# A grouped-query attention block with a cached K and V: TensorE's batches 8 to 31 as a hardware loop with counted-down semaphores and fixed buffer slots

## The chip, the cores and the metric

The kernel runs on one core of one Trainium2 chip. The metric is the device time of one execution in microseconds (us). Five runs of the kernel before took between 367.18 and 367.44 us, with a median of 367.32. A profile is one further execution; its span is the time from the first to the last instruction on the core.

The engines are named as in the profile: PE is TensorE's matmul row and PEld its weight loads, DVE is VectorE, ACT ScalarE, POOL GpSimd, and SP SyncE, whose queue issues the DMA transfers.

## The reference

```python
B, Sq, D, Hq, Hkv, Sk, Dh = 32, 4, 1024, 32, 4, 2048, 128
q = (x @ wq).reshape(B, Sq, Hq, Dh).transpose(0, 2, 1, 3)
k = jnp.repeat(k_cache, rep, axis=1)          # k_cache, v_cache: [B, Hkv, Sk, Dh]
v = jnp.repeat(v_cache, rep, axis=1)
scores = jnp.einsum("bhqd,bhkd->bhqk", q, k) * (Dh ** -0.5)
p = _softmax(scores, axis=-1)
o = jnp.einsum("bhqk,bhkd->bhqd", p, v)
return o.transpose(0, 2, 1, 3).reshape(B, Sq, Hq * Dh) @ wo
```

All tensors are bfloat16. Each batch has 2 MB of K and 2 MB of V; wq and wo have 8 MB each. With the 64 cache tiles that is about 151 MB read from memory, once.

## The kernel before, in words

The program is written as a list of operations for each engine (class `_Program`). Every operation may name what it waits for and what it completes. `emit` turns a wait into "semaphore of the producing engine at least n", where n is the producer's place in that engine's count: counters only ever rise, each engine has one, and each buffer slot has one for its DMA. `emit` writes every engine's stream straight out, so PE's code holds each matmul of all 32 batches.

Buffers. `big` has eight slots of 2 MB. At first four of them hold wq; then all K and V tiles run through the slots as a ring, in the order of the list `loads`: three K tiles ahead, then K of batch b+3 (b+4 from batch 17 on) and V of batch b in turn. A load waits for the last user of its slot: a K tile is free after its last transpose `("kt", b, 3)`, a V tile after its last matmul `("pv", b)`. From batch 10 on one slot is taken out of the ring and serves as a second P buffer (`PF_sb`), cleared by ACT; until then there is one (`PD_sb`). At the end the four chunks of wo use the slots that come free next. SP issues all loads in the order of the list, so a load that waits holds up all behind it.

Per batch i the work is:

- `qd` (L277, POOL): four copies put the queries of batch i in block-diagonal form into `QD_sb`;
- `kt` (L286, DVE): four transposes of K chunks into one of two halves of `KT_sb`;
- `pe_qk` (L298 for the matmul with a weight load, L16 for those that keep the weights): 16 matmuls into `ps_s`, which has one buffer, so they wait for `exp` of the batch before;
- `softmax_max` (L306, L307, DVE): the row maximum and its negative scaling;
- `softmax_exp` (L311, ACT): exp from `ps_s` into `P_sb`, with the row sum;
- `pt` (L319, L320, DVE): the transpose of P into `PT_sb` and the reciprocal of the sum;
- `pd` (L332, POOL): four copies into `PD_sb` or `PF_sb`, block-diagonal;
- `pe_pv` (L341, PE): 64 matmuls of P with V into `ps_r`, then `o_evac` (L348, ACT), `pe_ot` (L359, PE) and `ot_evac` (L364, ACT).

Iteration i of the main loop, which runs in Python and is written out in full, emits `qd` and two of the four `kt` chunks of batch i+1, QK and the maximum of batch i, exp, the other two `kt` chunks, `pt` of batch i, then PV matmuls of earlier batches up to `pv_until(i)`, and `pd` of batch i-1. `pv_until` lags one batch more from a certain batch on; the step is spread over four batches (`EASE`) that have 48 PV matmuls instead of 64. Before, these are batches 12 to 15 (`SW = 12`).

After the last batch come the output projection (`oproj`, L374 and L16) and the two output transfers.

Of the kernel before, what the change touches and what calls it, by code (L numbers as in the profile page):

```python
# [29 lines left out]
class _Program:  # L30
# [6 lines left out]
    def __init__(self):  # L37
        self.ops = {e: [] for e in self.ENGINES}
        self.count = {e: 0 for e in self.ENGINES}
        self.at = {}  # L40
        self.dma_count = {}
        self.last_pool = None

    def op(self, engine, emit, waits=(), done=None):
        if engine == "pool":
            done = done or ("pool", self.count["pool"])
            waits = tuple(waits) + (self.last_pool,) * (self.last_pool is not None)
            self.last_pool = done
        if done is not None:
            assert done not in self.at, done  # L50
            self.count[engine] += 1
            self.at[done] = (engine, self.count[engine])
        self.ops[engine].append((emit, tuple(waits), done is not None, None))

    def dma(self, engine, emit, waits, done, sem):
        assert done not in self.at, done
        self.dma_count[sem] = self.dma_count.get(sem, 0) + 16
        self.at[done] = (sem, self.dma_count[sem])
        self.ops[engine].append((emit, tuple(waits), False, sem))

    def emit(self, name, engine, sems):
        seen = {}
        for emit, waits, counted, dma_sem in self.ops[name]:
            need = {}
            for w in waits:
                s, n = self.at[w]
                if seen.get(s, 0) < n:
                    need[s] = max(need.get(s, 0), n)
            for s, n in need.items():
                engine.wait_ge(sems[s], n)  # L70
                seen[s] = n
            ins = emit(engine)
            if counted:
                ins.then_inc(sems[name], 1)
            if dma_sem is not None:
                ins.then_inc(sems[dma_sem], 16)


def bass_standalone__gqa_block_cached__sampling_kernel(
# [23 lines left out]
    SL = 17  # L103
    SW = 12
    SPB = 9
# [8 lines left out]
    with ExitStack() as es:  # L114
# [42 lines left out]
        for c in range(4):  # L157
            p.dma("sp", lambda e, c=c: e.dma_start(w_sb[:, 2 * c:2 * c + 2, :], wq_v[:, 2 * c:2 * c + 2, :]),  # L158
                  [], ("wq", c), f"s_b{c}")

        loads = [("k", b) for b in range(LEAD)]
        for b in range(B):
            ahead = [b + LEAD] if b < SL else [b + LEAD, b + LEAD + 1] if b == SL else [b + LEAD + 1]
            loads += [("k", a) for a in ahead if a < B] + [("v", b)]
        n_pd = loads.index(("k", SPB + LEAD))
        spare = (NW + n_pd) % NS
        pd_holder = loads[n_pd - NS]

        def ring_slot(n):
            if n < n_pd:  # L170
                return (NW + n) % NS
            return (spare + 1 + (n - n_pd) % (NS - 1)) % NS

        PF_sb = big[:, spare, :, :].rearrange("p t d -> p (t d)").rearrange("p (t g q w) -> p t g q w", t=T // 2, g=G, q=32)
        slot_of = {}
        holder = {s: "w" for s in range(NW)}
        for n, (kind, b) in enumerate(loads):
            s = ring_slot(n)
            before, holder[s], slot_of[kind, b] = holder.get(s), (kind, b), s
            waits = [] if before is None else ["qproj"] if before == "w" else [  # L180
                ("kt", before[1], NCH - 1) if before[0] == "k" else ("pv", before[1])]
            src = (k_cache if kind == "k" else v_cache)[b].rearrange("g (r t) d -> (g r) t d", r=R)
            p.dma("sp", lambda e, s=s, src=src: e.dma_start(big[:, s, :, :], src), waits, (kind, b), f"s_b{s}")
        n = len(loads)
        wo_slot = [ring_slot(n + c) for c in range(NW)]
# [6 lines left out]
        for c, m in enumerate(WO):  # L192
            assert h0 // 8 == (h0 + m - 1) // 8
            kind, b = holder[wo_slot[h0 // 8]]
            if m > 1:
                dst = wo_at(h0, m).rearrange("p (h n) -> p h n", n=2 * D)
                src = wo_v[:, h0 // 2:(h0 + m) // 2, :]
            else:
                dst, src = wo_at(h0, 1), wo_v[:, h0 // 2, h0 % 2 * D:(h0 % 2 + 1) * D]
            p.dma("sp", lambda e, dst=dst, src=src: e.dma_start(dst, src),  # L200
                [("kt", b, NCH - 1) if kind == "k" else ("pv", b)], ("wo", c), f"s_wo{c}")
            h0 += m
# [9 lines left out]
        p.op("pool", lambda e: e.memset(words(PD_sb[:, :, :, :, :].rearrange("p t g q w -> p (t g q w)")), 0.0), [], "pd0")  # L212

# [47 lines left out]
        freed = [("qe", m, 1) for m in range(4)]  # L261

        def slot(free):
            n = len(freed)
            freed.append(free)
            return ring[n % 4], [freed[n - 4]]
# [4 lines left out]
        def qd(i):  # L271
            for g in range(G):
                rows = slice(32 * g, 32 * (g + 1))
                src = words(QT_sb[rows, i, :, :, :, :].rearrange("p a h s w -> p a (h s w)"))
                dst = words(QD_sb[rows, i % 2, :, g, :, :].rearrange("p a q w -> p a (q w)"))
                waits = ["qd0"] + [("qe", m, a) for m in range(4) for a in range(2)] + ([("qk", i - 2)] if i > 1 else [])
                p.op("pool", lambda e, s=src, d=dst: e.tensor_copy(d, s), waits if g == 0 else [],  # L277
                     ("qd", i) if g == G - 1 else None)

        def kt(i, chunks):  # L280
            for c in chunks:
                ts = slice(TC * c, TC * (c + 1))
                src = words(big[:, slot_of["k", i], ts, :].rearrange("p t d -> p (t d)"))
                dst = words(KT_sb[:, i % 2, ts, :, :, :].rearrange("p t a r w -> p (t a r w)"))
                waits = [("k", i)] + ([("qk", i - 2)] if i > 1 else ["qt_all"] if i == 1 else [])
                p.op("dve", lambda e, s=src, d=dst: e.transpose(d, s), waits, ("kt", i, c))  # L286

        def pe_qk(i):
            waits = [("kt", i, NCH - 1), ("qd", i)] + ([("exp", i - 1)] if i else [("qs", j) for j in range(8)])
            for a in range(2):  # L290
                for w in range(2):
                    for c in range(NCH):
# [10 lines left out]
                        p.op("pe", mm, waits, ("qk", i) if last and c == NCH - 1 else None)  # L303
# [6 lines left out]
        def softmax_exp(i):  # L310
# [3 lines left out]
                [("negmx", i)] + ([("pt", i - 1)] if i else ["qproj"]), ("exp", i))  # L314

# [6 lines left out]
        def pd_of(i):  # L322
            return PF_sb if i > SPB and i % 2 else PD_sb

        def pd(i):
            free = [j for j in range(i) if pd_of(j) is pd_of(i)]
            free = ("pv", free[-1]) if free else "pd0" if pd_of(i) is PD_sb else "pf0"
            for g in range(G):
# [3 lines left out]
                p.op("pool", lambda e, s=src, d=dst: e.tensor_copy(d, s), [("pt", i), free], ("pd", i, g))  # L332

        def pe_pv(i, t):
            if t == 0:
                ring_of["o", i], waits = slot(("o", i))
                waits = waits + [("pd", i, g) for g in range(G)] + [("v", i)]
            else:
                waits = []
# [3 lines left out]
                rhs=big[:, slot_of["v", i], t, :], start=(t == 0), stop=(t == T - 1)),  # L343
                waits, ("pv", i) if t == T - 1 else None)

        def o_evac(i):
            buf = ring_of["o", i]
            p.op("act", lambda e: e.activation(o_sb[:, :], buf[:, 0:Dh], ACT.Copy, scale=rinv[:, i % 4:i % 4 + 1]),  # L348
                 [("pv", i), ("rinv", i)] + ([("oT", i - 1)] if i else []), ("o", i))

        def pe_ot(i):
            buf, waits = slot(("ot", i))
            ring_of["ot", i] = buf
            for e_ in range(2):
                for u in range(2):
# [4 lines left out]
                         waits + [("o", i)] if e_ == u == 0 else [], ("oT", i) if e_ == u == 1 else None)  # L360
# [8 lines left out]
        def oproj(c):  # L369
            for h in range(sum(WO[:c]), sum(WO[:c + 1])):  # L370
                for j in range(2):
# [7 lines left out]
                    p.op("pe", mm, [("wo", c), ("ot", B - 1), ("exp", B - 1)], ("op", j) if h == Hq - 1 else None)  # L379
# [10 lines left out]
        def pv_until(i):  # L390
            less = min(max(i - SW + 1, 0), EASE) * (T // EASE)
            return max((i - 1) * T - less, 0)
# [4 lines left out]
        for i in range(B + 2):  # L397
            upto = pv_until(i) if i < B else (i - 2) * T if i == B else B * T
# [7 lines left out]
            if i < B and j >= 0 and j not in ot_done:  # L406
                ot_done.append(j)
                pe_ot(j)
                ot_evac(j)
            if i < B:  # L410
                softmax_exp(i)
            if i == SPB:
                p.op("act", lambda e: e.memzero(words(PF_sb.rearrange("p t g q w -> p (t g q w)"))),
                     [("kt", pd_holder[1], NCH - 1) if pd_holder[0] == "k" else ("pv", pd_holder[1])], "pf0")
# [4 lines left out]
            for k in range(done, upto):  # L419
                pe_pv(k // T, k % T)  # L420
                if k % T == T - 1:
                    if i >= B and k // T - 1 not in ot_done:
                        ot_done.append(k // T - 1)
# [12 lines left out]
        names = list(p.ENGINES) + sorted({s for s in p.dma_count})  # L436
# [54 lines left out]
```

## Time and profile before

| what | value |
|---|---|
| median of five runs | 367.32 us (367.18 to 367.44) |
| the profiled execution | 367.1 us |
| its span | 365.3 us |
| PE busy | 283.2 us (78%), 2840 instructions |
| PEld busy | 138.5 us (38%), 2368 instructions |
| DVE busy | 271.7 us (74%) |
| ACT busy | 107.6 us (29%) |
| POOL busy | 166.7 us (46%) |
| DMA | 151.90 MB, mean 416 GB/s |

How to read the page: busy times are those of each engine, as shares of the span. Further on, the page cuts the span into 40 equal slices of 9.1 us; each digit is the busy share of a slice in tenths, 9 for 90% or more. The row PEclk is the clock that was granted to TensorE, the row DMA the mean busy share of the 16 DMA engines, the row GB/s what they moved. A timeline row has the start, the length, engine, line, operation, output and input; in brackets stands how long the engine was idle before, and what ended it. The costliest groups of the page, with count, busy time, mean length in ns, idle time before and its main releaser:

```profile
L286 DVE STREAM_TRANSPOSE KT_sb<-big 128x1024 f32<-128x1024 f32 x128 | 150.5, 1216 | 1.9 <-DMA big<-in_k_cache_dram 1.9
...
L311 ACT ACTIVATE P_sb<-ps_s,negmx 128x2048 bf16<-128x2048 f32 x32 | 81.4, 2545 | 95.7 <-DVE negmx L307 95.7
L298 PE MATMUL ps_s<-KT_sb,QD_sb 128*128 128x512 bf16 x128 | 51.3, 401 | 57.6 <-ACT P_sb L311 48.0
L306 DVE TENSOR_REDUCE mx<-ps_s 128x1 f32<-128x2048 f32 x32 | 73.3, 2291 | 21.0 <-PE ps_s L16 21.0
L341 PE MATMUL ps_r<-big,PD_sb 128*128 128x128 bf16 x1344 | 79.0, 219 | 4.2 <-DMA big<-in_v_cache_dram 3.5
```

### The profile page before, as it was taken

How to read it: one execution, taken by the hardware profiler on the slowest of the kernel's cores; microseconds unless marked ns; L12 is line 12 of the kernel's file. 1: busy time of each engine (PE TensorE's matmuls, PEld its weight loads, DVE VectorE, ACT ScalarE, POOL GpSimd, SP SyncE). 2: the span in 40 equal slices, each digit the busy share in tenths (PEclk: the TensorE clock that was granted, in tenths of full speed). 3: DMA queues.
4: the chain of work that ended last, by engine and by line, in shares of the span. 5: the costliest groups of instructions: out<-in, count | busy, mean ns of one | idle time of the engine just before them, and what ended most of it. 6: DMA issues, size and time to landing. Idle time of an engine off the chain costs nothing.

```text
span 365.3 us, 6105 instructions
## 1 busy us (share of the span) xinstructions
PE 283.2 (78%) x2840; PEld 138.5 (38%) x2368; DVE 271.7 (74%) x270; ACT 107.6 (29%) x135; POOL 166.7 (46%) x265
## 2 busy tenths in 40 slices
PE   1972557888888888768778888888888877889895
PEld 1002002444444444333224444444444433448721
DVE  0029677999999999997779999999999999753000
ACT  1010112333333373331333333333333333333100
POOL 5002150555555555852555555555555555446300
PEclk9998888999999999998889999999999999999999
DMA  8999999999999999999999999999999999999993
GB/s 328 431 431 429 429 422 429 431 429 430 422 427 429 423 429 426 423 429 427 431 429 425 427 428 422 425 427 429 429 429 423 429 420 427 429 427 422 405 405 123
DMA packets 12586, 151.90 MB, mean 416 GB/s; under 512 B 1296, under 2 KB 1552, under 8 KB 3856
## 3 DMA queue, kind: packets, MB, share of 16 engines
q1 hardware_dynamic: 12416, 151.39, 98.0%
q8 instruction: 20, 0.33, 0.4%
q10 hardware_dynamic: 144, 0.13, 0.1%
q14 instruction: 6, 0.05, 0.0%
HBM read 151.26 MB, written 0.26 MB: 415 GB/s over the span
## 4 chain that ended last, share of the span: by engine, by line
PE 37%; DVE 22%; ACT 19%; DMA 18%; issue 2%; POOL 2%; SPq 0%; POOLq 0%
PE ps_s L16 23%; ACT P_sb L311 18%; DVE mx L306 17%; PE ps_s L298 9%; DMA big<-in_v_cache_dram 7%; DMA big<-in_wq_dram 6%; DMA big<-in_wo_dram 5%; PE ps_r L341 4%; DVE KT_sb L286 2%; POOL PD_sb L332 2%; DVE negmx L307 1%; DVE QT_sb L258 1%; DVE KT_sb L242 1%; PE ps_s L374 1%; SPq L158 0%
## 5 line engine op out<-in xcount | busy, mean ns | idle before, releaser
L286 DVE STREAM_TRANSPOSE KT_sb<-big 128x1024 f32<-128x1024 f32 x128 | 150.5, 1216 | 1.9 <-DMA big<-in_k_cache_dram 1.9
L332 POOL COPY PD_sb<-PT_sb 32x1024 f32<-32x1024 f32 x84 | 86.8, 1033 | 92.0 <-PE ps_r L341 70.3
L16 PE MATMUL ps_s<-KT_sb,QD_sb 128*128 128x512 bf16 x384 | 111.3, 399 | 0.0
L311 ACT ACTIVATE P_sb<-ps_s,negmx 128x2048 bf16<-128x2048 f32 x32 | 81.4, 2545 | 95.7 <-DVE negmx L307 95.7
L298 PE MATMUL ps_s<-KT_sb,QD_sb 128*128 128x512 bf16 x128 | 51.3, 401 | 57.6 <-ACT P_sb L311 48.0
L306 DVE TENSOR_REDUCE mx<-ps_s 128x1 f32<-128x2048 f32 x32 | 73.3, 2291 | 21.0 <-PE ps_s L16 21.0
L341 PE MATMUL ps_r<-big,PD_sb 128*128 128x128 bf16 x1344 | 79.0, 219 | 4.2 <-DMA big<-in_v_cache_dram 3.5
L341 PEld LDWEIGHTS ps_r<-big,PD_sb 128*128 128x128 bf16 x1344 | 75.3, 98 | 7.0 <-DMA big<-in_v_cache_dram 3.7
L298 PEld LDWEIGHTS ps_s<-KT_sb,QD_sb 128*128 128x128 bf16 x128 | 12.9, 101 | 141.2 <-issue 77.7
L332 POOL COPY big<-PT_sb 32x1024 f32<-32x1024 f32 x44 | 45.5, 1033 | 40.3 <-PE ps_r L341 33.7
L319 DVE STREAM_TRANSPOSE PT_sb<-P_sb 128x1024 f32<-128x1024 f32 x32 | 39.9, 1245 | 14.4 <-ACT P_sb L311 14.4
L277 POOL COPY QD_sb<-QT_sb 32x64 f32<-32x64 f32 x128 | 29.4, 230 | 41.2 <-DVE QT_sb L258 25.5
L341 PE MATMUL ps_r<-big 128*128 128x128 bf16 x704 | 41.4, 219 | 4.1 <-DMA big<-in_v_cache_dram 3.5
L364 ACT ACTIVATE oT_sb<-ps_r 128x128 bf16<-128x128 f32 x32 | 8.9, 277 | 116.0 <-PE ps_r L359 116.0
L341 PEld LDWEIGHTS ps_r<-big 128*128 128x128 bf16 x704 | 39.4, 98 | 4.7 <-DMA big<-in_v_cache_dram 3.8
L382 DVE CAST P_sb<-ps_s 128x512 bf16<-128x512 f32 x1 | 0.7, 692 | 27.2 <-PE ps_s L374 27.2
L359 PEld LDWEIGHTS ps_r<-ident,o_sb 128*64 128x64 bf16 x128 | 4.6, 108 | 31.2 <-issue 29.0
L242 DVE CAST KT_sb<-ps_r 128x512 bf16<-128x512 f32 x2 | 1.3, 686 | 20.1 <-PE ps_r L226 20.1
L374 PE MATMUL ps_s<-big,oT_sb 128*128 128x512 bf16 x32 | 12.2, 380 | 1.7 <-DMA big<-in_wo_dram 1.2
L348 ACT ACTIVATE o_sb<-ps_r,rinv 128x128 bf16<-128x128 f32 x32 | 11.2, 351 | 3.3 <-PE ps_r L341 3.3
L16 PE MATMUL ps_s<-big,oT_sb 128*128 128x512 bf16 x32 | 12.1, 379 | 0.0
L16 PE MATMUL ps_s<-big,P_sb 128*128 128x512 bf16 x32 | 9.1, 410 | 0.0
(29 smaller groups left out, 60.3 us busy)
## 6 DMA issues: line engine op xcount, KB each, us to landing
big<-in_k_cache_dram SPq DMA_DIRECT2D x32, 2048.0 KB, 22.8
big<-in_v_cache_dram SPq DMA_DIRECT2D x32, 2048.0 KB, 21.4
big<-in_wq_dram SPq DMA_DIRECT2D x4, 2048.0 KB, 13.9
big<-in_wo_dram SPq DMA_DIRECT2D x7, 1024.0 KB, 27.2
big<-in_wo_dram SPq DMA_DIRECT2D x1, 512.0 KB, 17.1
big<-in_wo_dram SPq DMA_DIRECT2D x2, 256.0 KB, 14.7
P_sb<-in_x_dram SPq DMA_DIRECT2D x1, 256.0 KB, 2.7
out_dram<-P_sb SPq DMA_DIRECT2D x1, 128.0 KB, 1.8
```

Source lines behind the costliest of these rows:

```text
L16: return eng.add_instruction(mybir.InstMatmult(name=nc.get_next_instruction_name(), engine=eng.engine, start_tensor_calc=start, stop_tenso ...
L277: p.op("pool", lambda e, s=src, d=dst: e.tensor_copy(d, s), waits if g == 0 else [], ("qd", i) if g == G - 1 else None)
L286: p.op("dve", lambda e, s=src, d=dst: e.transpose(d, s), waits, ("kt", i, c))
L298: mm = lambda e, a_=(out_, lhsT, rhs), f=first, l=last: e.matmul(a_[0], lhsT=a_[1], rhs=a_[2], start=f, stop=l, skip_group_check=True)
L306: p.op("dve", lambda e: e.tensor_reduce(mx[:, i % 4:i % 4 + 1], ps_s[:, :], AX.X, ALU.max), [("qk", i)], ("mx", i))
L311: p.op("act", lambda e: e.activation(P_sb[:, :, :, :].rearrange("p t r w -> p t w r"), ps_s[:, :].rearrange("p (t w r) -> p t w r", w=2, r=R),
L319: p.op("dve", lambda e: e.transpose(dst, src), [("exp", i)] + ([("pd", i - 2, G - 1)] if i > 1 else []), ("pt", i))
L332: p.op("pool", lambda e, s=src, d=dst: e.tensor_copy(d, s), [("pt", i), free], ("pd", i, g))
L341: p.op("pe", lambda e: e.matmul(buf[:, 0:Dh], lhsT=pd_of(i)[:, t // 2, :, :, t % 2].rearrange("p g q -> p (g q)"), rhs=big[:, slot_of["v", ...
L348: p.op("act", lambda e: e.activation(o_sb[:, :], buf[:, 0:Dh], ACT.Copy, scale=rinv[:, i % 4:i % 4 + 1]), [("pv", i), ("rinv", i)] + ([("o ...
L364: p.op("act", lambda e: e.activation(oT_sb[:, :, :, i * Sq:(i + 1) * Sq].rearrange("p h e s -> p e h s"), buf[:, 0:128].rearrange("p (e h ...
L374: mm = lambda e, a=(out_, lhsT, rhs), h=h: e.matmul(a[0], lhsT=a[1], rhs=a[2], start=(h == 0), stop=(h == Hq - 1), skip_group_check=True)
```

## The change

PE's code for iterations 8 to 31 becomes a hardware loop (`Fori`) whose body has four batches and runs six times. For that, all four-batch parts of PE's list must be the same, addresses and waits included:

- **Waits.** Inside the loop PE can't wait for a rising count. Five new semaphores, `t_kt`, `t_qd`, `t_exp`, `t_pd` and `t_o`, are raised by one by the producer and counted down by PE, in an instruction of its own that waits and subtracts (`takes`). PE takes V's DMA semaphore in the same way, 16 at a time. The last `kt` chunk of a batch and `o_evac` raise their `t_` semaphore in place of their engine's counter (`gives=`); who else waits for them now waits for the next counted instruction of that engine (`late`). `qd`, `exp` and `pd` keep the engine's counter and are followed by a `give`: the engine waits for its own counter and then raises the semaphore. PE's waits for the `ps_r` ring are dropped.
- **Slots.** V of batch b lies in slot b mod 4, K of batch b in slot 4 + b mod 3. Slot 7 is the second P buffer from the start, cleared by POOL, and batches use the two P buffers in turn from batch 0 on.
- **Order of the loads.** Up to batch 7 V stands ahead of K of three batches on, from batch 8 (`S1`) behind it; from batch 14 (`S2`) K is four batches on.
- **Lag of PV.** `SW` is 4, so batches 4 to 7 are the eased ones.
- **wo.** Its chunks go into the slots of K 29, K 30, K 31 and V 28.
- wq's chunks have semaphores of their own, and the tail handles one batch of PV in each of the iterations 32 to 34.

```diff
+    def give(self, engine, after, gives):
+        self.ops[engine].append((None, (after,), (), (gives, 1)))
...
+                for s, n in takes:
+                    engine.wait_ge(sems[s], n).then_inc(sems[s], -n)
...
+        marks = self.loop
+        parts = [ops[a:b] for a, b in zip(marks, marks[1:])]
...
+        run(ops[:marks[0]])
+        with engine.Fori(0, len(parts)):
+            run(parts[0])
+        run(ops[marks[-1]:])
...
-    SL = 17
-    SW = 12
-    SPB = 9
+    S1 = 8
+    S2 = 14
+    VS = 4
+    KS = 3
+    SW = 4
...
         for b in range(B):
-            ahead = [b + LEAD] if b < SL else [b + LEAD, b + LEAD + 1] if b == SL else [b + LEAD + 1]
-            loads += [("k", a) for a in ahead if a < B] + [("v", b)]
...
+            ahead = b + LEAD + (b >= S2)
+            ks = [("k", a) for a in range(len(loads) - b, ahead + 1) if a < B]
+            loads += [("v", b)] + ks if b < S1 else ks + [("v", b)]
+
+        def slot_of(kind, b):
+            return b % VS if kind == "v" else VS + b % KS
...
+            waits = ["qproj"] * (b < VS) if kind == "v" else []
+            if kind == "v" and b >= VS:
+                waits = [("pv", b - VS)]
+            if kind == "k" and b >= KS:
+                waits = [("kt", b - KS, NCH - 1)]
...
+        wo_for = [("k", B - 3), ("k", B - 2), ("k", B - 1), ("v", B - 4)]
...
+        p.op("pool", lambda e: e.memset(words(PF_sb.rearrange("p t g q w -> p (t g q w)")), 0.0), [], "pf0")
...
+            p.give("pool", ("qd", i), "t_qd")
...
-                p.op("dve", lambda e, s=src, d=dst: e.transpose(d, s), waits, ("kt", i, c))
+                p.op("dve", lambda e, s=src, d=dst: e.transpose(d, s), waits, ("kt", i, c), gives="t_kt" if c == NCH - 1 else None)
...
-            waits = [("kt", i, NCH - 1), ("qd", i)] + ([("exp", i - 1)] if i else [("qs", j) for j in range(8)])
+            waits = [] if i else [("qs", j) for j in range(8)]
+            takes = [("t_kt", 1), ("t_qd", 1)] + [("t_exp", 1)] * (i > 0)
...
+            if i < L:
+                p.give("act", ("exp", i), "t_exp")
...
-            return PF_sb if i > SPB and i % 2 else PD_sb
+            return PF_sb if i % 2 else PD_sb
...
+            free = ("pv", i - 2) if i > 1 else ("pd0", "pf0")[i]
...
+            p.give("pool", ("pd", i, G - 1), "t_pd")
...
+                takes = [("t_pd", 1), (f"s_b{slot_of('v', i)}", 16)]
...
-            return max((i - 1) * T - less, 0)
+            return max((i - 1) * T - less, 0) if i < B else (i - 2) * T
...
-            if i == SPB:
-                p.op("act", lambda e: e.memzero(words(PF_sb.rearrange("p t g q w -> p (t g q w)"))),
-                     [("kt", pd_holder[1], NCH - 1) if pd_holder[0] == "k" else ("pv", pd_holder[1])], "pf0")
...
+        p.loop = starts[SW + EASE:B + 1:4]
```

## The prediction, on record before the changed kernel ran

> **What bounds the kernel now.** I read the page's slices first, then the DMA part, then the queue waits of SyncE, and last the timeline of one iteration.
>
> ```profile
> DMA  8999999999999999999999999999999999999993
> GB/s 328 431 431 429 429 422 429 431 429 430 422 427 429 423 429 426 423 429 427 431 429 425 427 428 422 425 427 429 429 429 423 429 420 427 429 427 422 405 405 123
> ...
> q8 instruction: 20, 0.33, 0.4%
> ...
> big<-in_k_cache_dram SPq DMA_DIRECT2D x32, 2048.0 KB, 22.8
> big<-in_v_cache_dram SPq DMA_DIRECT2D x32, 2048.0 KB, 21.4
> ```
>
> The DMA row is full in every slice but the first and the last: the 151 MB set the end, and compute matters only where it lets the queue run dry. A load lands 21 to 23 us after its issue, so four to five loads of 2 MB lie in the queue.
>
> ```profile
> SPq L183 <- DVE KT_sb L286: 200.2, 30, 10.1
> ...
> 23.23 0.39 PE L226 MATMUL ps_r<-big,P_sb 128*128 128x512 bf16 x1 [1.28 <-DMA big<-in_wq_dram]
> ...
> 321.11 3.58 PEld L341 LDWEIGHTS ps_r<-big 128*128 128x128 bf16 x64 [2.50 <-DMA big<-in_v_cache_dram]
> ```
>
> The first row is from SP's waits, the others are from the timeline. SP mostly waits for a K slot that a transpose (L286) frees. The other two rows give the pace: the last wq chunk lands at 23.2; V of batch 27, load 60 of the 64 K and V loads, at 321.1 (V of 26, load 58, ended a like wait at 311.3). So load N lands at 23.2 + 4.965 N, and a batch of two takes 9.93 us.
>
> ```profile
> 247.85 2.36 DVE L286 STREAM_TRANSPOSE KT_sb<-big 128x1024 f32<-128x1024 f32 x2
> ...
> 250.24 0.33 SPq L183 DMA_DIRECT2D big<-in_v_cache_dram  x1
> ...
> 250.59 1.25 DVE L319 STREAM_TRANSPOSE PT_sb<-P_sb 128x1024 f32<-128x1024 f32 x1 [0.38 <-ACT P_sb L311]
> ...
> 250.70 0.38 PE L298 MATMUL ps_s<-KT_sb,QD_sb 128*128 128x512 bf16 x1 [1.42 <-ACT P_sb L311]
> ```
>
> One batch of compute is a ring: QK, max, exp (here from 247.97), QK again. Maxima start 8.91 us apart in nearly all batches, 1.02 less than the DMA's 9.93. In the last row PE has idled 1.42 us for exp. Three batches are slower:
>
> ```profile
> 160.38 2.29 DVE L306 TENSOR_REDUCE mx<-ps_s 128x1 f32<-128x2048 f32 x1 [0.22 <-PE ps_s L16]
> ...
> 165.61 0.38 PE L298 MATMUL ps_s<-KT_sb,QD_sb 128*128 128x512 bf16 x1 [2.59 <-ACT P_sb L311]
> ...
> 170.96 2.29 DVE L306 TENSOR_REDUCE mx<-ps_s 128x1 f32<-128x2048 f32 x1 [1.90 <-PE ps_s L16]
> ```
>
> Batches 12 to 15 run 48 PV matmuls instead of 64 (EASE). PE then idles 2.3 to 2.6 us, and after three of those four gaps QK ran at a granted clock of 0.83: periods of 10.58, 10.57 and 10.44, together S = 4.9 us more than 3 x 8.91. The full queue hid it.
>
> **The change, part by part.** I call the moment at which pt of batch b (L319) ends E(b). In the trace it is 6.37 us after the start of that batch's maximum, so E(b) = 77.6 + 8.91 (b - 3) without extra time; E(0), E(1), E(2) are 47.9, 58.3 and 68.7.
>
> *The loads.* Before, the transpose of K(b+1) released one K and one V load at once (250.24 above). After, K(b+4) waits for the last chunk of K(b+1), which now counts up t_kt and no longer DVE's own counter; SP is released by the next counted DVE instruction, pt of batch b: 251.84 instead of 250.24, 1.6 us later. Behind it in SP's queue stands a V, whose own wait (PV four batches back) is then over. So each E(b) releases a pair, and the queue must not drain between two of them. Counting the load list, issued before E(b) are: 6, 8, 10, 12, 14 loads for b = 0 to 4; 19 for b = 7, where K11 is moved ahead of V8 (S1); 21 for b = 8; 31 for b = 13; 32 for b = 14, where K17 and K18 stand ahead of V14 (S2); 34 for b = 15, and so on by two. A new load needs 2.1 us until its data lands beyond its own transfer (x: issued 0.74, used 3.44, 0.26 MB at 431 GB/s is 0.6), and 0.1 for SP: 2.2. The idle time of the DMA by E(b), against an uninterrupted queue, is thus
>
> D(b) = E(b) + 2.2 - (23.2 + 4.965 N).
>
> At the head it is negative: 68.7 + 2.2 - 72.85 = -2 at b = 2, the tightest. Without extra time D(7) = 113.2 + 2.2 - 117.5 = -2.1, D(8) = -3.1, D(14) = 175.6 + 2.2 - 182.1 = -4.3, and then 1.02 lower per batch. Before, one load more was queued, 5 us of cover. What compute loses now counts once it exceeds these few microseconds.
>
> *Easing moved from batches 12-15 to 4-7 (SW).* The same four gaps, the same S, but now ahead of b = 8. Bounds: no slow batch, 0; four, 6.5. I take the three seen, 4.9, of which 3.3 lie before E(7).
>
> [...] The rows above show gaps of 2.30 to 2.59 followed by the slow clock. [...]
>
> *Semaphores.* exp no longer releases QK itself: ACT waits for its own counter, then raises t_exp, and PE takes it in an instruction of its own. Behind ACT's wait stands only o_evac, which has slack. The new hop and take are not in the trace. Nearest rows: negmx ends 247.93, exp starts 247.97 (0.04); exp's accumulator read ends 250.55, QK starts 250.70 (0.15). One to two more hops: 0.09 to 0.30 per batch; I take 0.2, between them. The takes of t_kt, t_qd, t_pd, t_o and of V's counter are raised earlier and cost nothing while PE idles 1.4 us for exp. The same gives on POOL stand ahead of pd; POOL is busy 46%, so nothing.
>
> *The back edge.* Six passes (batches 8 to 31), five taken branches, at the ends of batches 11, 15, 19, 23, 27. What a branch back over some 640 PE instructions costs, X, no row shows. The 20 instruction packets (16 KB each, about one for 260 of PE's 5208 matmuls and weight loads) show that code is streamed. From below, X = 0, if the loop stays in the engine. From above: a fetch like x's, 2.7 us from issue to use, and a packet's time (0.4% of 16 x 365.3 us over 20, 1.2), so 3.9, plus a slow QK after the long gap, 1.66, so 5.5. I take x's 2.7 less PE's idle 1.4, X = 1.3.
>
> [...]
>
> *The rest.* Clearing the second P buffer moves from ACT to POOL before the first QD copy (31.4 us; POOL is free from 6 us, the clearing of the first took 3.51): nothing, and if the cover were gone, 3.5. K3 waits for a transpose chunk at 37, while the queue holds loads to 43: nothing. At the tail wo waits for pt of batches 28 to 30 and PV of 28, all past before V31's transfer has ended (load 64, 341): nothing. The order of V28 to V31 and wo is unchanged.
>
> *Sum.* D(7) = -2.1 + 3.3 + 1.4 = 2.6. D(8) = -3.1 + 4.9 + 1.6 = 3.4. D(14) = -4.3 + 4.9 + 14 x 0.2 + 1.3 = 4.7. D(16), with two edges, = -6.3 + 4.9 + 3.2 + 2.6 = 4.4; later ones are smaller. The largest counts, since a full queue never makes time up: 4.7 us. The profiled execution took 367.1 in all (span 365.3 and 1.8 around it), 0.2 below the median of 367.32: 367.1 + 4.7 = **371.8**. With the small ends (two slow batches, 0.09, X = 0) D(8) = 0.9; with four slow ones and 0.30, D(14) = 7.8: 368 to 375.
>
> **Rivals.**
>
> *The back edge becomes the bound (slower still).* Four batches leave 4 x (1.02 - 0.2) = 3.3 us per pass. If X exceeds that, every pass loses more. For it: code is streamed, and the gap would grow past the 2.3 us that already cost the clock. Against: 1.4 us of idle cover it. With 3.9 - 1.4 + 1.66 = 4.1, D(28) = -18.6 + 4.9 + 5.6 + 5 x 4.1 = 12.4: 379.5; at 5.5 it is 386.
>
> *The queue covers it.* If the eased gaps don't throttle, D(14) = -4.3 + 2.8 + 1.3 is below 0: 367.1. For it: the batch after the first eased one ran fast, and a gap of 1.70 us at 67.6 too. Against: three of four were slow.
>
> *Faster: fewer instruction packets.* The loop's 640 instructions stay resident, twelve of 20 packets vanish, and S is 0. Slices range from 431 to 420 GB/s; the mean of the full ones is some 427, 1% below the best, 3.5 us over the span. If all of that were the 20 packets, twelve are worth 2.1: 365. It decides only if D stays below 2. Against: 0.4% of DMA time is little, and dips need not be packets.
>
> **How the numbers follow.** Forecast 0.56 (368 to 377), back edge 0.21 (above 377), covered 0.13 (366.6 to 368), fewer packets 0.10. A difference of 0.2%, 0.73 us, is about what a measurement of this kernel can tell from none. Faster 0.10, same 0.13, slower 0.77. The range 366.5 to 381 leaves out most of the fewer-packets case and the upper half of the back edge's.
>
> **What would show it.** Right: DMA digits below 9 near 115 to 130 us and near 175 to 205; K landing 8 to 15 us after issue instead of 22.8; a clock of 0.83 over three periods between 90 and 130; maxima about 9.1 apart otherwise, every fourth a little more. Wrong: a DMA row as full as now with the slow periods present (the 2.2 or the count of loads is off); maxima over 12 us apart at each back edge (first rival); far fewer than 20 packets on q8 with more GB/s (third). The forecast falls if QK stays fast after the eased batches, or if the branch costs over 3.3.

## The result, and the profile after

The changed kernel took 368.62 us (median of 28 runs, 366.85 to 370.36), the kernel before 367.38 in 48 runs beside it (367.17 to 367.83): the ratio is 1.0035 with a 95% interval of 1.0026 to 1.0044. It is slower by 1.24 us where 4.4 was forecast, and its times spread over 3.5 us where those of the kernel before spread over 0.7. The profiled execution took 369.81 (span 368.0), 1.2 above the median; it shows 2.7 us more than the profile before.

From the page of the changed kernel, the DMA rows over the slices (9.2 us each), the queues, and the issues (count, KB each, median us from issue to landing):

```profile
PEclk9998668999889999999999999999999989989999
DMA  8999999999997999999999999999999999999993
GB/s 338 431 427 427 427 427 410 399 425 425 426 427 312 399 422 427 427 426 429 427 429 426 433 426 427 427 431 429 427 429 429 427 429 426 431 427 422 406 406 139
...
q8 instruction: 8, 0.13, 0.1%
...
big<-in_k_cache_dram SPq DMA_DIRECT2D x32, 2048.0 KB, 12.8
big<-in_v_cache_dram SPq DMA_DIRECT2D x32, 2048.0 KB, 17.0
```

The DMA row has one hole, 312 GB/s in the slice from 110 to 120 us. Against 427 in its neighbours that is (427 - 312) / 427 x 9.2 = 2.5 us of idle queue, and 0.6 more in the slice behind it. A shallow dip (410 and 399 GB/s, from 55 to 74 us, at E(2)) adds 1.0, so the queue idles for 4.1 us in all. Nothing dips between 130 us and the tail. K now lands 12.8 us after its issue instead of 22.8: less is queued. And only 8 packets of instructions were fetched on q8 instead of 20.

The hole seen closer, in four windows (length; busy us and count of PE, PEld, DVE, ACT, POOL; granted clock; DMA share; GB/s):

```profile
90.00:101.00 11.00, 8.37 (x67) 3.24 (x52) 8.69 (x9) 2.94 (x3) 5.05 (x8) 0.84 1.00 425
101.00:112.00 11.00, 8.66 (x77) 3.63 (x64) 8.53 (x9) 3.27 (x5) 5.05 (x8) 0.84 1.01 432
112.00:121.00 9.00, 6.66 (x72) 3.27 (x58) 8.34 (x9) 3.28 (x5) 5.05 (x8) 1.00 0.72 273
121.00:130.00 9.00, 7.53 (x88) 4.15 (x74) 8.32 (x9) 3.27 (x5) 4.82 (x7) 1.00 1.01 430
```

Two periods ran at a clock of 0.84, and the queue went dry just after them. The timeline of the same stretch:

```profile
95.94 0.51 PE L323 MATMUL ps_s<-KT_sb,QD_sb 128*128 128x512 bf16 x1 [2.63 <-PEq L85]
...
101.28 2.29 DVE L332 TENSOR_REDUCE mx<-ps_s 128x1 f32<-128x2048 f32 x1 [1.94 <-PE ps_s L16]
...
106.56 0.59 PE L323 MATMUL ps_s<-KT_sb,QD_sb 128*128 128x512 bf16 x1 [2.34 <-PEq L85]
...
107.67 10.80 SPq L206 DMA_DIRECT2D big<-in_k_cache_dram  x2
...
111.75 2.29 DVE L332 TENSOR_REDUCE mx<-ps_s 128x1 f32<-128x2048 f32 x1 [1.79 <-PE ps_s L16]
...
116.87 1.25 DVE L347 STREAM_TRANSPOSE PT_sb<-P_sb 128x1024 f32<-128x1024 f32 x1 [0.36 <-ACT P_sb L337]
...
117.03 0.38 PE L323 MATMUL ps_s<-KT_sb,QD_sb 128*128 128x512 bf16 x1 [2.34 <-PEq L85]
...
118.52 0.43 SPq L206 DMA_DIRECT2D big<-in_v_cache_dram  x1
...
120.69 2.29 DVE L332 TENSOR_REDUCE mx<-ps_s 128x1 f32<-128x2048 f32 x1 [0.27 <-PE ps_s L16]
...
129.65 2.29 DVE L332 TENSOR_REDUCE mx<-ps_s 128x1 f32<-128x2048 f32 x1 [0.27 <-PE ps_s L16]
...
138.62 2.29 DVE L332 TENSOR_REDUCE mx<-ps_s 128x1 f32<-128x2048 f32 x1 [0.27 <-PE ps_s L16]
...
147.58 2.29 DVE L332 TENSOR_REDUCE mx<-ps_s 128x1 f32<-128x2048 f32 x1 [0.27 <-PE ps_s L16]
...
156.55 2.29 DVE L332 TENSOR_REDUCE mx<-ps_s 128x1 f32<-128x2048 f32 x1 [0.27 <-PE ps_s L16]
```

The SPq row issues K10 at 107.67, then K11, put ahead of V8 by `S1`. K11 has to wait until pt of batch 7 has ended (116.87 + 1.25 = 118.12), and V8 goes out behind it at 118.52. In the trace's DMA completion events the last load ahead of these two landed at 118.8 and K11 at 125.9, 7.1 us later instead of the undisturbed 4.9. PE's gaps of 2.63 and 2.34 us were followed by slow QKs; a further one of 2.34 us, at 117.03, by a fast one. The last five rows are the maxima of batches 8 to 12: 8.96 or 8.97 us apart, within a pass of the loop and from 147.58 to 156.55 across its first branch back.

The costliest groups (count, busy us, mean ns, idle before, releaser) stand as before but for one: the maximum waits 25.1 us for QK instead of 21.0, the sum over the slow QKs, the late head and the tail:

```profile
L310 DVE STREAM_TRANSPOSE KT_sb<-big 128x1024 f32<-128x1024 f32 x128 | 150.6, 1216 | 1.7 <-DMA big<-in_k_cache_dram 1.5
...
L332 DVE TENSOR_REDUCE mx<-ps_s 128x1 f32<-128x2048 f32 x32 | 73.3, 2292 | 25.1 <-PE ps_s L16 24.9
```

Last, the end. In this execution the output projection starts when the last batch is ready:

```profile
350.96 0.38 PE L400 MATMUL ps_s<-big,oT_sb 128*128 128x512 bf16 x1 [0.46 <-ACT oT_sb L390]
```

Its 64 matmuls then run on without waiting for wo, and the span ends 17.0 us after this row. In the kernel before the projection started at 346.45 and waited for three chunks of wo; its span ended 4.25 us after the last wo chunk had landed (361.06). So there are two ends: the DMA's (the last wo chunk plus 4.25) and PE's (start of the projection plus 17.0), and the later one sets the time. Here they are close together: the last chunk landed at 363.36, so the DMA's end would have come at 367.6, PE's came at 368.0.

### The profile page after: what moved, and what is told of

Same layout as the page of the kernel before. It is cut to its first block, busy times and chain, and to the rows that moved or that the text cites. A ratio compares the mean times of both kernels' runs of the same rounds, so it can differ in the third digit from the quotient of the medians.

```text
span 368.0 us, 6351 instructions
## 1 busy us (share of the span) xinstructions
PE 286.0 (78%) x2840; PEld 141.7 (39%) x2368; DVE 271.9 (74%) x270; ACT 107.1 (29%) x134; POOL 170.2 (46%) x266
## 5 line engine op out<-in xcount | busy, mean ns | idle before, releaser
L359 POOL COPY PD_sb<-PT_sb 32x1024 f32<-32x1024 f32 x64 | 66.1, 1034 | 70.0 <-PE ps_r L368 56.8
L359 POOL COPY big<-PT_sb 32x1024 f32<-32x1024 f32 x64 | 66.1, 1034 | 62.6 <-PE ps_r L368 50.8
L332 DVE TENSOR_REDUCE mx<-ps_s 128x1 f32<-128x2048 f32 x32 | 73.3, 2292 | 25.1 <-PE ps_s L16 24.9
L368 PE MATMUL ps_r<-big 128*128 128x128 bf16 x1024 | 61.7, 222 | 6.6 <-PEq L85 6.6
L368 PE MATMUL ps_r<-big,PD_sb 128*128 128x128 bf16 x1024 | 61.7, 222 | 6.5 <-PEq L85 6.5
L368 PEld LDWEIGHTS ps_r<-big,PD_sb 128*128 128x128 bf16 x1024 | 59.0, 99 | 9.0 <-issue 8.3
L368 PEld LDWEIGHTS ps_r<-big 128*128 128x128 bf16 x1024 | 59.0, 100 | 7.4 <-issue 7.0
## 6 DMA issues: line engine op xcount, KB each, us to landing
big<-in_k_cache_dram SPq DMA_DIRECT2D x32, 2048.0 KB, 12.8
```

The source lines that it names most:

```text
L332: p.op("dve", lambda e: e.tensor_reduce(mx[:, i % 4:i % 4 + 1], ps_s[:, :], AX.X, ALU.max), [("qk", i)], ("mx", i))
L368: p.op("pe", lambda e: e.matmul(buf[:, 0:Dh], lhsT=pd_of(i)[:, t // 2, :, :, t % 2].rearrange("p g q -> p (g q)"), rhs=big[:, slot_of("v", ...
```

## The experiments

The theory: (1) the queue runs dry at E(7), because K11 stands ahead of V8 while PE's clock falls in the eased batches; (2) the loop itself costs nothing; (3) staying in the loop saves instruction packets, and that gives part back. The rivals: the loss comes from the semaphores and the loop; from the moved `kt` counter; or from the second step, `S2`. Each of them was undone or doubled alone. The edits are against the changed kernel; the kernel before took 367.30 to 367.33 us beside them.

**E1: the step in the order of loads comes after the eased batches.**

```diff
-    S1 = 8
+    S1 = 12
```

> S1 = 12 instead of 8: V stands ahead of K up to batch 11, so one load more is queued at E(7) to E(10), and the step to 27 loads comes at E(11). Theory 'drained queue': the changed kernel's 2.7 us more of span are the idle DMA between 112 and 121 us, D(7) = 118.1 + 2.1 - 117.5 = 2.7. With 20 loads instead of 19 D(7) = -2.3, and D(11) = 154.0 + 2.1 - 157.3 = -1.2: the gap is gone, no slice under 395 GB/s after the first, time 366.5 to 367.4 (at or under the kernel before). Rival 'loop and semaphores': the time is lost in the takes, gives and back edges, which are all still there: 368.6 as for the changed kernel, and the slow QKs change nothing.

Measured: 366.53 us (365.83 to 369.51, 12 runs), 2.1 below the changed kernel by the medians and 1.4 by the means; against the kernel before 0.9998 (0.9977 to 1.0020). The page's DMA row and instruction queue:

```profile
GB/s 327 430 432 432 425 430 428 432 427 427 428 426 423 426 423 426 433 430 428 381 428 431 425 425 432 428 432 426 426 428 432 428 426 429 428 428 424 402 409 155
...
q8 instruction: 8, 0.13, 0.1%
```

The hole is gone although two QKs were slow as before (here those of batches 6 and 8); a small one of 1.0 us, 381 GB/s, is left at the second step. The changed kernel with the same two QKs slow is E12 below, and it has a hole. So the step's place made the hole, and the slow QKs alone don't. The upper end of the runs was a miss: five of the twelve still took 368.1 to 369.5.

**E2: no abrupt easing: the step of the PV lag spread over eight batches from 0 on, 56 PV matmuls instead of 48.**

```diff
-    SW = 4
-    EASE = 4
+    SW = 0
+    EASE = 8
```

> SW = 0 and EASE = 8: the step of the PV lag is spread over batches 2 to 7 and the batch before them, 56 PV matmuls in each instead of four batches with 48; order of the loads and loop are those of the changed kernel. Theory 'drained queue': PE's gap ahead of QK falls from 2.3 to 2.6 us to about 1.9 us, QK stays fast, E(7) comes 3.2 us earlier, D(7) = 114.9 + 2.1 - 117.5 = -0.5, so at most a trace of the gap stays: 366.6 to 367.6, and the spread of the runs shrinks from 3.5 us to under 1. If 1.9 us already throttle, more QKs are slow and the time is 370 or more. Rival 'loop and semaphores': 368.6.

Measured: 368.37 (366.32 to 369.80, 11 runs), ratio to before 1.0024 (1.0007 to 1.0041): a miss. The first batches now had even less PE work, one of them 40 PV matmuls, and the QK behind it was slow (a period of 10.44). The queue ran dry earlier instead:

```profile
GB/s 332 432 434 430 428 421 407 387 398 384 432 427 416 421 414 428 427 430 428 428 428 427 428 427 428 428 428 428 428 428 428 428 428 427 428 430 420 402 409 137
```

Slices 6 to 9 (from 0) hold 407, 387, 398 and 384 GB/s: the same kind of loss, at E(2) and E(3). The head has as little cover (work left in the queue) as E(7). The five QKs behind batches with 56 matmuls were fast, after gaps of PE of 1.90 to 2.19 us.

**E3: the six passes written out instead of looped, all else equal.**

```diff
-        with engine.Fori(0, len(parts)):
-            run(parts[0])
+        for part in parts:
+            run(part)
```

> The six passes are written out one after the other instead of the hardware loop; waits, counted-down semaphores, slots and order of the loads are those of the changed kernel. Theory 'drained queue': the loop costs nothing (maxima 8.96 us apart also across the back edges), the gap near 115 us stays; the code's packets come back, 20 instead of 8, which by the lowest runs (366.85 against 367.17) is worth 0 to 0.5 us: 368.6 to 369.1. Rival 'loop and semaphores', where the back edge costs: 367.4 to 368, faster than the changed kernel by 0.6 or more.

Measured: 369.98 (368.53 to 372.41, 6 runs), ratio 1.0075 (1.0049 to 1.0101).

```profile
GB/s 337 429 426 427 429 431 420 396 411 428 426 426 310 415 424 436 427 426 426 424 427 427 427 423 431 426 426 427 427 431 424 424 429 428 424 429 419 404 405 114
...
q8 instruction: 21, 0.34, 0.4%
```

The hole is there without any branch (310 GB/s in the same slice), the packets are back, and the kernel is 1.36 us slower than with the loop. So the loop doesn't cost time, it saves some; the saving was larger than the expected 0 to 0.5 us.

**E4: the last `kt` chunk keeps DVE's own counter, and a give follows it.**

```diff
-  p.op("dve", ..., waits, ("kt", i, c), gives="t_kt" if c == NCH - 1 else None)
+  p.op("dve", ..., waits, ("kt", i, c))
+  if c == NCH - 1:
+      p.give("dve", ("kt", i, c), "t_kt")
```

> The last kt chunk keeps DVE's own counter and a give raises t_kt behind it, as qd, exp and pd do: SP is again released by the chunk itself and not by pt, 1.6 us earlier in every batch. Everything else is the changed kernel. Theory 'drained queue': E(7) moves from 118.1 to 116.5, D(7) from 2.7 to 1.1 with two slow QKs and to below 0 with one; the partial gap at E(2) (70.2 us) goes too. 366.3 to 367.6, about 1.5 us under the changed kernel. Rival 'loop and semaphores' (one more hop on the busiest vector engine): 368.6 or slower.

Measured: 367.75 (366.08 to 368.83, 12 runs), 0.9 below the changed kernel, less than expected; ratio to before 1.0010 (0.9998 to 1.0023). A later release of the loads is a part of the loss, then, not the whole.

```profile
GB/s 330 431 431 429 429 429 423 427 427 427 427 429 336 429 427 429 431 430 429 423 427 429 427 425 425 429 431 431 431 429 431 427 425 430 424 429 422 403 410 160
```

In this profile the same two QKs were slow as in the changed kernel's first one, those of batches 6 and 7. The hole is 1.9 us instead of 3.1, and the dip at E(2) is gone.

**E5: the second step moved up, as a dose: one K more stands ahead of a V while cover is short.**

```diff
-    S2 = 14
+    S2 = 9
```

> S2 = 9 instead of 14: K stands four batches ahead already from batch 9, so one load less is queued at E(9) to E(13). This doubles the suspected cost. Theory 'drained queue': N at E(9) is 22 instead of 23, D(9) = 136.0 + 2.1 - 132.4 = 5.7 with two slow QKs, 4.1 with one, against 2.7 and 1.0 at E(7) without the edit: 370.5 to 373, slower than the changed kernel by about 3 us, with a second gap near 138 us. Rival 'loop and semaphores': 368.6.

Measured: 371.97 (371.04 to 373.20, 4 runs), ratio 1.0136 (1.0122 to 1.0151), 3.4 over the changed kernel.

```profile
GB/s 334 431 428 426 426 426 431 419 425 434 422 428 376 385 240 426 427 435 428 426 431 427 428 425 428 431 430 428 430 428 426 430 428 427 428 430 428 402 408 173
```

Slices 12 to 14 now hold 376, 385 and 240 GB/s: (51 + 42 + 187) / 427 x 9.2 = 6.0 us of idle queue instead of 3.1, and the time goes up by 3.4, as expected. A load that waits ahead of one that could go is what empties the queue.

**E6: easing over eight batches, 4 to 11, with 56 PV matmuls each.**

```diff
-    EASE = 4
+    EASE = 8
```

> SW = 4 and EASE = 8: batches 4 to 11 have 56 PV matmuls, none before is cut, the loop runs from batch 12 in five passes. The run with SW = 0 showed QK fast after every batch with 56, and one slow QK after the batch with 40. Theory 'drained queue': no slow QK after batch 3, E(7) at 114.9 at the latest, D(7) = -0.5 or less: 366 to 367.2, and no run above 368. If the gap at E(7) stays all the same, the throttled QKs were not what made it. Rival 'loop and semaphores': 368.6.

Measured: 366.79 (365.92 to 368.94, 12 runs), ratio 1.0003 (0.9984 to 1.0021). In the profile PE's gap before QK is some 1.9 us in the eased batches, one QK is slow (batch 9) and no slice between the first and the tail is below 423 GB/s:

```profile
GB/s 322 432 430 428 432 432 423 430 426 424 425 427 428 428 427 425 427 427 428 428 425 429 425 429 428 425 430 428 428 432 427 428 428 426 430 427 427 401 407 141
```

The hole thus needs both the step and the slow QKs ahead of it, as E1 and this run each take one of them away. Four of twelve runs took 368.8 to 368.9, where none above 368 was expected.

**E7 and E8: all three remedies (S1 = 12, EASE = 8, `kt` with its own counter), looped and written out.**

```diff
-    S1 = 8
-    EASE = 4
+    S1 = 12
+    EASE = 8
```

and the edit of E4; E8 also has that of E3.

> The three edits together: S1 = 12, EASE = 8 with SW = 4, and K released by its own chunk; loop and counted-down semaphores stay. Theory 'drained queue, and fewer code packets': the queue never runs dry after the head; what is left against the kernel before is 8 code packets on q8 instead of 20. In the kernel before the slowest of the 16 DMA engines falls behind by 1.1 to 1.5 us three times, each time at a code packet; here once: 365.0 to 366.2, faster than before by 1.2 to 2.3 us, spread under 1 us. If packets don't matter: 367.1 to 367.6, the time before. Rival 'loop and semaphores': 368 or more.

> The same three edits, with the passes written out instead of the loop: only PE's code and its packets on q8 (20 or 21 instead of 8) differ from e7_all. If the packets cost what the late landings of the kernel before suggest: 366.8 to 367.6, slower than e7_all by 1.2 to 2.3 us. If not: equal to e7_all within 0.3 us. If the back edge costs, it is faster than e7_all.

Measured: E7 366.49 (365.58 to 368.34, 12 runs), ratio 0.9984 (0.9969 to 1.0000); E8 367.43 (367.23 to 369.53, 12 runs), ratio 1.0011 (0.9998 to 1.0024). E7's page:

```profile
GB/s 327 432 430 423 432 432 428 432 425 430 425 423 425 426 430 426 429 423 428 430 425 425 430 432 425 430 423 432 428 428 430 430 430 426 422 428 424 404 407 133
...
q8 instruction: 11, 0.18, 0.2%
```

E8's:

```profile
GB/s 330 432 430 430 428 427 423 428 427 428 428 428 425 428 427 425 427 427 428 427 428 421 427 427 428 425 425 427 427 428 428 427 430 427 422 428 418 406 401 118
...
q8 instruction: 21, 0.34, 0.4%
```

Both rows are full. With E3 this makes a table of two by two, medians in us:

| | loop | written out | loop saves |
|---|---|---|---|
| with the hole | 368.62 | 369.98 (E3) | 1.36 (13 packets fewer) |
| without it | 366.49 (E7) | 367.43 (E8) | 0.94 (10 packets fewer) |
| the hole costs | 2.13 | 2.55 | |

With 6 to 28 runs each, a difference in this table is sure to about 1 us; by the means the loop saves 1.7 (with the hole) and 1.0 us. That is about 0.1 us a packet in both rows, if all of it comes from the packets. The completion events point to them: in E8 the last of the 16 transfers of a load falls back by 1.2 us three times, in E7 by 1.5 us twice. At the third time in E8 (load 57, landed at 306.5 us) an instruction packet is moved at 304.3; in E7 none moves between 185.0 and 341.1. The last wo chunk lands at 361.4 in E8, at 359.7 in E7.

E8 has every part of the change (`kt` in E4's form) but the loop and the hole, and stands near the time of the kernel before: the added semaphores, takes and gives together cost 0.9 us at most, the upper end of its interval. E7 is the best version found; it is clearly faster than the changed kernel, since its interval lies apart from 1.0026 to 1.0044, but against the kernel before it ends at 1.0000. It missed its expectation: 365.0 to 366.2 us in all runs, with a spread under 1.

**E9 and E10: the second step left out, K three batches ahead throughout (E9 on E7, E10 on the changed kernel).**

```diff
-    S2 = 14
+    S2 = 32
```

> The three edits of e7_all and S2 = 32, so K stays three batches ahead of V in the list to the end, and each of the last V tiles but those after K31 comes one load (4.9 us) earlier. Theory 'two ends': beside the DMA's end there is PE's own tail, 64 projection matmuls of 14 us that start after the last batch; in e7_all PE waits 2.4 us and more for V in batches 29 to 31, throttles, and starts the projection at 347.4 us with 0.3 us of waits for wo left, so its runs above 367 are such tails. With V earlier the tail starts before 346.5, PE waits for wo again, and the time is that of the DMA: 365.2 to 366.2 in all runs, spread under 1 us. If the slow runs of e7_all come from the DMA, the spread stays at 2.5 us or more.

> The changed kernel with S2 = 32 alone. Theory 'drained queue': the gap at E(7) stays (19 loads), 2 to 3 us of DMA with two slow QKs, 0 to 1 with one; PE's late tail goes. The slowest runs (370) come down to about 369, the fast ones stay: median 367.6 to 368.3. If the tail alone made the loss: 366.3 and no slow runs. If neither matters: 368.6.

Measured: E9 368.48 (368.41 to 370.06, 6 runs), ratio 1.0040 (1.0027 to 1.0053); E10 372.11 (369.76 to 373.74, 6 runs), ratio 1.0129 (1.0098 to 1.0160). Both were expected to be faster than what they were made from, and both were slower, by 2.0 and 3.5 us. E9's page:

```profile
GB/s 322 438 434 427 425 429 425 429 422 429 425 427 427 427 427 427 428 425 427 427 425 425 429 429 429 427 429 429 427 427 429 425 429 426 429 426 417 407 387 53
...
L310 DVE STREAM_TRANSPOSE KT_sb<-big 128x1024 f32<-128x1024 f32 x128 | 150.8, 1217 | 7.8 <-DMA big<-in_k_cache_dram 7.7
```

The DMA row is full, and the last wo chunk lands at 359.7 us as in E7, yet the kernel ends later. Each K tile now stands behind one V more, DVE waits for it (7.7 us in all instead of 2.5 in E7), and the last batches are ready late. The projection started at 347.39 in E7; here are E9's and E10's:

```profile
349.52 0.38 PE L402 MATMUL ps_s<-big,oT_sb 128*128 128x512 bf16 x1 [0.46 <-ACT oT_sb L392]
...
352.59 0.38 PE L400 MATMUL ps_s<-big,oT_sb 128*128 128x512 bf16 x1 [0.46 <-ACT oT_sb L390]
```

349.52 + 17.0 is 366.5, and E9's span 366.6. 352.59 + 17.0 is 369.6, and E10's span 369.7, while its last wo chunk had landed at 361.1. This is the other end: a full queue isn't enough, K must also come early enough for the last batches. The step `S2` is needed. Both expectations knew of PE's end, but reckoned only with V coming earlier and not with K coming later.

**E11 and E12: the changed kernel itself, two more profiles.**

> The changed kernel again, one more profile. Theory 'drained queue': with E(7) read from its maxima, D(7) = E(7) + 2.1 - 117.5 tells how long the DMA stands near 115 us. With n slow QKs in batches 4 to 7 it is about -2.1 + 1.6 n plus what the first three batches lose. Where it is below 0.5, load 64 lands before 341 us.

> The changed kernel again, as e11_look: another draw of which QKs are throttled, the same relation between E(7), the gap and the landing of load 64; and the projection's start against its waits for wo tells which of the two ends set the span.

Measured: 367.37 and 367.63 us, one execution each. E11:

```profile
GB/s 332 432 434 427 427 427 416 427 428 431 425 430 364 394 412 414 428 429 432 423 430 426 430 428 430 428 428 427 430 428 430 427 427 422 430 428 428 400 410 178
```

And E12:

```profile
GB/s 324 432 435 430 425 426 425 428 427 429 426 428 399 401 412 425 429 432 428 412 430 431 430 425 430 428 428 428 426 428 426 430 426 427 428 430 422 402 410 126
```

The same slice holds 364 GB/s in E11 and 399 in E12 (312 in the first profile), and the slow QKs of both are those of batches 6 and 8 instead of 6 and 7. So the second slow QK can no longer delay E(7), and the hole is smaller: 2.7 and 1.5 us of idle queue over slices 12 to 15, where the first profile has 3.2. The first maximum started at 41.64 and 41.21 instead of 42.36. In both the projection starts by 346.9 and waits for wo. Which batches are slow, and how late the head is, changes from execution to execution, and the profile with the largest hole is the longest: 369.81 us against 367.37 and 367.63. Between E11 and E12 the order is the other way round. E11's expectation puts D(7) at -0.2 and -1.1 here, and yet the queue ran dry in both, so the idle time is larger than that formula says; why, stands below under the pace.

## Why the prediction was right and wrong

**Bound by the DMA queue, loss only where it runs dry: right for the loss that was forecast.** E1 and E5 move it with the order of loads alone. E9 and E10 show a second bound, PE's end, that the forecast put at nothing.

**E(7), D(7) = 2.6: right in place, near in size, partly by luck.** The forecast has E(7) at 113.2 + 3.3 + 1.4 = 117.9; it came at 118.1, and K11 landed 2.2 us late. S before E(7) was 10.61 + 10.47 - 2 x 8.91 = 3.3 as forecast in this execution, but not in E11 and E12, where one of the two slow QKs came later. The 1.4 for the semaphores was 0.35 at most, and in its place the head was late: the maximum of batch 2 started at 63.84 instead of 62.33. The head itself, put at -2, also ran dry for some 1.0 us.

**The largest term, D(14) = 4.7: the step that failed.** Its parts, as sized and as measured:

- X = 1.3 for a back edge: 0. The maxima are 8.97 apart across it, and E3 is slower without it. The 1.3 and the upper end, 5.5, were the author's estimates for a fetch at each branch, worked out from x's 2.7 us between issue and use. No run shows such a fetch: after 144.0 us, in the first pass, the next instruction packet on q8 moves at 340.3. The low end, X = 0, is what was measured.
- 0.2 per batch for hop and take: 0.05, the difference of 8.96 and 8.91, below the low end of 0.09. Over 14 batches the forecast had 2.1 us too much.
- S = 4.9: 3.3 in this profile, since two of the four gaps, the first and the last, were followed by a fast QK.

With these and the head's 1.5 us D(14) is -4.3 + 3.3 + 0.7 + 1.5 = 1.2; from the trace, with E(14) at 180.87, it is 180.87 + 2.2 - 182.1 = 1.0. That is below D(7), so the queue doesn't run dry a second time, and no slice after 130 us dips. The loss of 4.7 at D(14) that the forecast counts didn't take place.

**The gain from fewer packets: left out of the sum.** It stood as a rival with at most 2.1 us for twelve; the loop's saving in the 2 x 2 table is 0.94 and 1.36. A rival that doesn't exclude the forecast belongs in its sum. Put together: 2.1 to 2.6 us for the hole less 0.9 to 1.4 is 0.7 to 1.7, and 1.24 was measured. The first profile, with its 4.1 us of idle queue, is a longer execution than most (369.81 against the median of 368.62); E11 and E12 had 2.9 and 1.8.

**The pace, 4.965 us a load: it contained the packets.** By the completion events of the 64 loads, undisturbed ones land 4.90 us apart, and the last of the 16 transfers of a load falls back by 1.2 to 1.5 us in three places of the kernel before, each where an instruction packet is moved. As a mean the pace was right; read as the speed of the queue it hid what the loop would save. It also hid how dry the queue gets. With 23.0 + 4.90 N in the forecast's own formula, and the release of K(b+4) taken from the traces in place of E(b), the largest D up to the tail fits the idle time that the GB/s rows show (slices under 420 against 427, in us) to 0.8 us:

| | changed | E11 | E12 | E1 | E2 | E3 | E4 | E5 | E6 | E7 |
|---|---|---|---|---|---|---|---|---|---|---|
| largest D at 4.90 a load | 4.2 | 2.2 | 1.2 | 1.1 | 2.9 | 4.0 | 1.9 | 6.3 | below 0 | below 0 |
| idle by the GB/s row | 4.1 | 2.9 | 1.8 | 1.0 | 3.4 | 4.0 | 1.9 | 6.2 | 0 | 0 |

**What was to show it.** K's landing after 12.8 us, a clock of 0.84 (in two periods, not three) and the dip near 115 were there. The dip from 175 to 205 was not, nor the maxima 9.1 apart, nor a longer fourth.

**The tail at nothing: not quite.** In the first profile PE's end came last: two PV batches ran slowly (periods of 11.32 and 11.40 near the end), and the projection started at 350.96. It ended 2.7 us later than the profile before, while the last wo chunk landed 2.3 later (363.4 and 361.1): PE's end added 0.4.

**Open.** E1, E6 and E7 still have runs of 367.4 to 369.5. E9, E10 and the first profile point to a late projection as the cause, but none of those runs was profiled, so it isn't shown. Nor is it shown that the whole of the loop's saving comes from the packets. They took 22.1 us in E3 and 8.3 in the changed kernel, which over 16 DMA engines is 0.9 us less, for 1.36 measured; the margin of about 1 us leaves open whether that is more than their share.

## What to carry to other kernels

When a full DMA queue sets the time, list for each moment of release how many loads stand ahead of it, and never put a load that must wait ahead of one that can go in a stage where compute is late; then look at the second end, the tail of compute after the last data. Cost a hardware loop by what it really fetches, and put its saving of instruction packets into the sum, not only its branch.

## What the runs showed that was not expected

- In six passes over some 640 PE instructions no packet moved on q8 after 144.0 us, in the first pass, until 340.3: 8 packets of 16 KB in all; 11 in E7, where four more batches stand ahead of the loop, and 21 in E3 and E8.
- Five counted-down semaphores a batch cost 0.05 us of an 8.91 us period, and the taken branch nothing that shows: the periods are 8.96 to 8.97 across it, and the same in E3, which has no branch.
- The clock fell after gaps of PE of 2.3 to 2.6 us, but not after all of them. In E1 four eased batches in a row show it (timeline, the first matmul of QK; in brackets the gap before it):

```profile
84.86 0.38 PE L323 MATMUL ps_s<-KT_sb,QD_sb 128*128 128x512 bf16 x1 [2.33 <-PEq L85]
...
93.80 0.59 PE L323 MATMUL ps_s<-KT_sb,QD_sb 128*128 128x512 bf16 x1 [2.63 <-PEq L85]
...
104.29 0.38 PE L323 MATMUL ps_s<-KT_sb,QD_sb 128*128 128x512 bf16 x1 [2.35 <-PEq L85]
...
113.22 0.38 PE L323 MATMUL ps_s<-KT_sb,QD_sb 128*128 128x512 bf16 x1 [2.34 <-PEq L85]
```

The first and the third QK were fast (periods of 8.94 us), the second and the fourth slow (10.48 and 10.62; the fourth begins at full clock and slows down within). The gap's length alone doesn't decide. In E6, with gaps of 1.90 to 2.19 us, one QK of eight was slow.

What decides can be read from the traces' clock records. In the first profile of the changed kernel and in the profile before, the clock is halved for 3.41 us at a time, or for 6.83, and all its changes in one execution lie on a grid of windows of 3.41 us. In the former (window; length, busy us and count of PE, granted clock, DMA share, GB/s):

```profile
92.64:96.05 3.41, 0.78 (x13) 1.00 1.01 428
96.05:99.47 3.42, 3.42 (x9) 0.50 0.99 422
102.88:106.29 3.41, 1.34 (x24) 1.00 0.99 423
106.29:109.70 3.41, 3.14 (x8) 0.50 1.02 437
113.12:116.53 3.41, 1.56 (x29) 1.00 0.93 394
116.53:119.94 3.41, 2.91 (x14) 1.00 0.39 101
```

PE idled for 2.63 and 2.07 us in the windows ahead of the two slow QKs. The gap of 2.34 us ahead of the fast QK at 117.03 was cut by a window's edge, at 116.53, into 1.85 and 0.50. In these two profiles, from 60 to 340 us, each of the seven windows at full clock with at least 2.06 us of idle PE is followed by one at half clock, and none with 1.92 us or less is. So here the idle time within one window decides, and the gap of 2.34 us that an edge divides was followed by a fast QK. The grid lies elsewhere in each of three executions of the changed kernel (the first halved window starts at 34.61 us in the first profile, at 33.09 in E11 and 32.06 in E12). So the slow QKs differ from one execution to the next.
